# Correcting a planner's dependency and small-copy times in an attention-plus-Fourier kernel

## The chip, the cores and the metric

The kernel runs on one core of one Trainium2 chip. The metric is the device time of that core in microseconds, the median of several executions. One more execution was recorded by the hardware profiler; all rows of the trace come from that one.

## The reference

Two independent sublayers share the sequence length 2048 and the width 448, and their outputs stand side by side.

```python
# A: Fourier mixing, real part
a = jnp.einsum("bsd,ed->bse", x, dft_hid_re)
b = jnp.einsum("bsd,ed->bse", x, dft_hid_im)
y = jnp.einsum("ts,bse->bte", dft_seq_re, a) - jnp.einsum("ts,bse->bte", dft_seq_im, b)
# B: multi-head attention, H = 16 heads of 28
qkv = (x @ wqkv) ...                       # q, k, v by head
scores = jnp.einsum("bhqd,bhkd->bhqk", q, k) * 28 ** -0.5
p = softmax(scores, axis=-1)
o = einsum("bhqk,bhkd->bhqd", p, v) ... @ wo
return jnp.concatenate([y, o], axis=-1)
```

All is float32. To keep the precision, most operands are split into a rounded part (`hi`) and a rest (`lo`), and a product is made as hi x hi + lo x hi + hi x lo.

## The kernel before

**Two kinds of work on TensorE.** *Fill* work is all that has no softmax in it: the projections of q and k (`project`) and of v (`values`), matmuls of L547; the Fourier sublayer's hidden DFT (`hidden`, L547 too, twice: real and imaginary) and its sequence DFT (`sequence`, L662, 2 x 16 row tiles of 48 matmuls). *Attention* works in units of one head and 512 queries, 64 in all. A unit's 16 score tiles of 128 x 512 are made by L808 (`unit_kept`, 44 units) or twice by L754 and L786 (`unit_twice`, 20 units). P times V is L735, in narrow tiles of 32 columns, two groups a unit; L877 folds four partial sums in the same narrow mode.

**A unit of `unit_kept`.** ScalarE (ACT) copies each score tile out of PSUM (L415); VectorE (DVE) runs an elementwise maximum over the 16 tiles, each reading the last one's result (L815, then L818). Behind them stands a short dependent chain on VectorE: a transpose (L823), a reduction (L825), three 32x16 copies (L830), a small reduction (L835), two more small copies (L833) and a transpose (L841). ScalarE copies the result to SBUF as `mb` (L843); the pairs of score tiles are shifted by it, on GpSimd (POOL) or VectorE (L858), ScalarE takes the exponential (L862), and L735 multiplies by V. The sum leaves PSUM for `ou` by either ScalarE (L415) or VectorE (L417). In `unit_twice` VectorE reduces each tile to row maxima (L758, L762), a transpose on TensorE (L717) and two small operations (L766, L767) send the maxima through DRAM into two extra rows of q, and the second set of scores (L786) goes straight into the exponential (L790).

**Weight pieces.** `Piece` loads 256 KB of a weight or DFT matrix (L515, on the SP queue) into one of three `wraw` buffers; ScalarE casts it to `whi` (L516), GpSimd subtracts to get `wlo` (L522). `project`, `hidden` and `sequence` each make their pieces that way. Projection results are emptied from two fill banks by ScalarE (L588) and VectorE (L589); values by VectorE (L615), stored by L619.

**What sets the order.** Nothing is scheduled on the chip by time: every engine runs its instructions in the order in which they were emitted. That order comes from a planner in the kernel itself (`Schedule`). It plays the kernel through with a guessed cost for each operation: each engine, when free, takes the ready task with the smallest key (a due time), if its buffers are free. The constants that matter here: `DVE_P` 0.60 for a full VectorE operation, `SMALL` for the small copies of L830 and L833, `RAW` (passed as `own`) for the extra time until a VectorE operation that reads the last one's result may start, and for a DMA its size and an `extra` latency. A piece's key is the due time of its first matmul less a lead (9 for `hidden`, 12 for `sequence`, 12 for the projections). A changed constant changes the emitted order of all engines, and nothing else.

Of the kernel before, what the change touches and what calls it, by code (L numbers as in the profile page):

```python
# [47 lines left out]
def f32(ap):  # L48
    return ap.bitcast(F32)
# [4 lines left out]

RAW = 0.16
LANES = 8
FLOW, FLOW_IN = 200.0, 400.0
T_IN = 20.0  # L60
# [257 lines left out]
def tile_kernel(ctx, tc, xa, wre, wim, wd, xb, wqkv, wo, out):  # L318
    nc = tc.nc
# [67 lines left out]


    M512, M448, MS = 0.2335, 0.2065, 0.2365
    ACT_P, ACT_S, DVE_P, POOL_2, SMALL = 0.48, 0.52, 0.60, 1.25, 0.11  # L390

    def pe(key, emit, n=1, d=MS, lat=0.25, **kw):
        return sch.add({"PE": n * d}, key, emit, lat=lat, **kw)
# [1 line left out]
    def dma(key, emit, size=256, extra=0.0, n=1, **kw):  # L395

        return sch.add({"SP": 0.4}, key, lambda e: emit(), dmas=[(size, extra)] * n, **kw)
# [111 lines left out]
    class Piece:  # L509


        def __init__(self, src, key, kind="c", early=False):
            self.hi, self.lo = whi.slot(), wlo.slot()
            raw = wraw.slot()
            ld = dma(key, lambda: nc.sync.dma_start(raw.t, src()), acq=[raw])  # L515
            a = act(key + (0 if early else 1), lambda: nc.scalar.activation(self.hi.t, raw.t, AF.Copy), ACT_S,  # L516
                    deps=[ld], acq=[self.hi], use=[raw])
            at = key + (0 if early else 1.5)
            both = ("DVE",) if early else ("POOL",)
            e = {g: {"DVE": 0.8, "POOL": 1.25}[g] for g in both}  # L520
            n = 4 if kind == "c" else 3
            b = sch.add(e, at, lambda g: eng[g].tensor_tensor(  # L522
                self.lo.t[:, :n], raw.t[:, :n], f32(self.hi.t)[:, :n], op=ALU.subtract),
                deps=[a], acq=[self.lo], use=[raw, self.hi])
            self.ready, self.hi_ready, self.lo_ready = [b], a, [b]
            if kind == "x":
                self.ready.append(sch.add({g: {"DVE": 0.3, "POOL": 0.53}[g] for g in both}, at, lambda g: eng[g].tensor_tensor(
                    self.hi.t[64:, 3], raw.t[64:, 3], f32(self.hi.t)[64:, 3], op=ALU.subtract),
                    deps=[a], use=[raw, self.hi]))
            elif kind == "w":  # L530
                self.ready.append(sch.add({g: {"DVE": 0.3, "POOL": 0.53}[g] for g in both}, at, lambda g: eng[g].tensor_tensor(
                    self.lo.t[:64, 3], raw.t[:64, 3], f32(self.hi.t)[:64, 3], op=ALU.subtract),
                    deps=[a, b], use=[raw, self.hi, self.lo]))
                self.ready.append(sch.add({"DVE": 0.15, "POOL": 0.25}, at, lambda g: eng[g].memset(
                    f32(self.lo.t)[64:, 3], 0.0), deps=[b], use=[self.lo]))
                self.lo_ready = self.ready
# [89 lines left out]
    def hidden(part, weights, ready, after):  # L626
        done = []
        for st in range(NT):
            key = fkey(11, M448)
            w = Piece(lambda st=st: xa[st], key - 9, "x")  # L630
            o = fill_s.slot()
            seq = products(lambda k, w=w: (lambda: w.hi.t[:, k]), lambda k, w=w: (lambda: w.lo.t[:, k]),
                           lambda w=w: (lambda: w.hi.t[:, 3]), lambda k: (lambda: weights.h[:, k]), lambda k: (lambda: weights.l[:, k]))
            end = chain(key, seq, o, D, [*w.ready, *ready], [w.hi, w.lo], M448, weights.slots if st == NT - 1 else ())
            hi, lo = ab_h[:, st, :], ab_l[:, st, :]
            if part == 0:
                a = act(key - 10, lambda o=o, hi=hi: nc.scalar.activation(hi, o.t[:, :D], AF.Copy), 0.43, deps=[end, *after], use=[o])
                b = dve(key - 10, lambda o=o, hi=hi, lo=lo: nc.vector.tensor_tensor(
                    lo, o.t[:, :D], f32(hi), op=ALU.subtract), 0.54, deps=[a], use=[o])
            else:  # L640
                a = act(key - 10, lambda o=o, hi=hi: nc.scalar.activation(hi, o.t[:, :D], AF.Copy, scale=-1.0), 0.43,
                        deps=[end, *after], use=[o])
                b = dve(key - 10, lambda o=o, hi=hi, lo=lo: nc.vector.scalar_tensor_tensor(
                    lo, o.t[:, :D], -1.0, f32(hi), op0=ALU.mult, op1=ALU.subtract), 0.54, deps=[a], use=[o])
            done.append(b)
        return done

    def sequence(part, made):
        src = wim if part else wre
        for tt in range(NT):  # L650
            o, pair = fill_s.slot(), kept_s.slot()
            yo = Half(pair, 0)
            begun = None
            for q in range(4):
                key = fkey(12, M448)
                w = Piece(lambda tt=tt, q=q: src[tt, :, q * 4:q * 4 + 4, :], key - 12)
                for i in range(12):
                    k, j = divmod(i, 3)

                    def emit(e, k=k, j=j, q=q, w=w, o=o):  # L660
                        a, b = ((w.hi, ab_h), (w.hi, ab_l), (w.lo, ab_h))[j]
                        nc.tensor.matmul(o.t[:, :D], a.t[:, k, :], b[:, q * 4 + k, :], start=(q == 0 and k == 0 and j == 0),  # L662
                                         stop=(q == 3 and k == 3 and j == 2))
                    first = q == 0 and i == 0
                    deps = [last[0]]
                    if i == 0:
                        deps += w.ready
                    if tt == 0:
                        deps += [made[q * 4 + k]]
                    last[0] = pe(key + i * M448, emit, d=M448, deps=deps, acq=[o] if first else [],  # L670
                                 use=[w.hi, w.lo, *([] if first else [o])])
                    if i == 0 and q == Q_YO:
                        begun = last[0]
            key = key - 10
            if part == 0:
                b = dve(key, lambda o=o, yo=yo: nc.vector.tensor_copy(yo.t[:, :D], o.t[:, :D]), 0.53, deps=[last[0]], use=[o, pair])
                y_stored[tt] = dma(key, lambda yo=yo, tt=tt: nc.sync.dma_start(y_d[tt], yo.t[:, :D]), deps=[b], use=[pair])
            else:
                ld = dma(key - 15, lambda yo=yo, tt=tt: nc.sync.dma_start(yo.t[:, :D], y_d[tt]), deps=[y_stored[tt], begun], use=[pair])
                b = dve(key, lambda o=o, yo=yo: nc.vector.tensor_tensor(yo.t[:, :D], o.t[:, :D], yo.t[:, :D], op=ALU.add), 0.53,  # L680
                        deps=[last[0], ld], use=[o, pair])
                dma(key, lambda yo=yo, tt=tt: nc.sync.dma_start(out[tt * P:(tt + 1) * P, 0:D], yo.t[:, :D]), deps=[b], use=[pair])
# [112 lines left out]
    def unit_kept(u):  # L795
# [6 lines left out]
        for kt in range(NT):  # L802
# [11 lines left out]
            if kt == 1:  # L814
                prev = dve(key - 20, lambda o=o, s=kept[0]: nc.vector.tensor_tensor(rm.t, o.t, s.t[:, 0, :], op=ALU.max),  # L815
                           deps=[m, cs[0]], use=[rm, o, kept[0]], lock=[o], own=RAW)
            elif kt:
                prev = dve(key - 20, lambda o=o: nc.vector.tensor_tensor(rm.t, o.t, rm.t, op=ALU.max),  # L818
                           deps=[m, prev], use=[rm, o], lock=[o], own=RAW)
        key = t_a + 16 * dt - 20  # L820
# [4 lines left out]
        r = dve(key, lambda o=o: nc.vector.tensor_reduce(  # L825
            pm.t[:, :NT], o.t.rearrange("p (j r) -> p j r", r=32), axis=AX.X, op=ALU.max, negate=True), deps=[t], use=[o, pm], own=RAW)

# [4 lines left out]
        def back(n, o=o):  # L832
            return lambda: nc.vector.tensor_copy(o.t[n:2 * n, :NT], o.t[:n, :NT])  # L833
        r = [dve(key, beside(i), SMALL, deps=[r], use=[pm], own=RAW) for i in (1, 2, 3)]
        r = dve(key, lambda o=o: nc.vector.tensor_reduce(  # L835
# [81 lines left out]
    key = fkey(0, 0)  # L917
# [5 lines left out]
    key = fkey(0, 0)  # L923
# [19 lines left out]
    for n, c in enumerate(LAST):  # L943
        raws = []
        for k in range(4):
            pair = kept_s.slot()
            raw = Half(pair, 0)
            key = T_OUT + n
            deps = [o_done[h, c] for h in range(H) if (h + 1) * DH > k * P and h * DH < (k + 1) * P] + [before["ka"]]
            if k < 3:  # L950
                ld = dma(key, lambda raw=raw, k=k, c=c: nc.sync.dma_start(raw.t, on_d[k * P:(k + 1) * P, c * CH:(c + 1) * CH]),
                         deps=deps, use=[pair])
            else:
# [3 lines left out]
                ld = dma(key, twice, 128, n=2, deps=deps, use=[pair])  # L957
            raws.append((raw, ld))
        for i in range(2):
            x = [kt_s.slot() for _ in range(4)]  # L960
            ready = []
            for k in range(4):
                raw, ld = raws[k]
                src = lambda raw=raw, i=i: raw.t[:, i * HF:(i + 1) * HF]
# [3 lines left out]
                key = T_OUT + n + i / 2  # L968
# [7 lines left out]
            for t in range(2):  # L976
# [6 lines left out]
                key = T_OUT + 5 + (n * 4 + i * 2 + t) * 2.3  # L983
# [49 lines left out]
```

## Time and profile before

| | us |
|---|---|
| median of 3 runs | 1163.07 (1162.79 to 1165.32) |
| profiled execution, its own time | 1163.75 |
| its span | 1161.9 |
| busy: TensorE, VectorE, ScalarE, GpSimd | 1145.3, 1010.8, 1029.1, 884.6 |

A row of the profile names the line of the kernel, the engine, the operation, what it writes and reads, and how often; then the busy time, the mean duration in ns and the engine's idle time ahead of it, with what ended that. PE is TensorE's matmul, PEld its weight load, which runs ahead of the matmul. In timeline rows the first number is the start and the second the duration, in microseconds from the span's start. A matmul's duration includes the time it takes to drain; the next one starts before it ends. GpSimd's spans are rough.

### The profile page before, as it was taken

To read this page: it belongs to the slowest core of one execution; us is meant where nothing else is said; L and a number is where in the kernel's file an instruction comes from. 1 tells how busy PE (TensorE), PEld (TensorE's weight loads), DVE (VectorE), ACT (ScalarE), POOL (GpSimd) and SP (SyncE) were. 2 spreads that over 40 slices of the span, in tenths; PEclk is the share of its full clock that TensorE was granted. 3 is DMA by queue.
4 is the path that set the end of the run, shared out by engine and by line. 5 is a ranking of instruction groups with operands and counts; after the bars stand their busy time and mean duration, and the time that the engine had idled before them with its cause. 6 is when DMAs were issued, how large, how long until landed. Compare 5 with 4: busy or idle time off the path is not lost.

```text
span 1161.9 us, 19485 instructions
## 1 busy us (share of the span) xinstructions
PE 1145.3 (99%) x6110; PEld 778.7 (67%) x6110; DVE 1010.8 (87%) x1803; ACT 1029.1 (89%) x1748; POOL 884.6 (76%) x521
## 2 busy tenths in 40 slices
PE   8999999999999999999999999999999999999998
PEld 7876556656676667767666656566666667766677
DVE  6599989999898989999899999998989998799832
ACT  5269999999999899999899999999999999899952
POOL 2138687888789888978888897987989899596630
PEclk9999999999999999999999999999999999999999
DMA  8893344222223222232333232232423223323543
GB/s 259 176 214 120 125 140 148 66 83 73 82 85 102 85 85 82 73 114 78 89 105 100 86 96 65 85 101 90 120 80 96 88 87 114 120 73 92 162 158 109
DMA packets 111880, 125.19 MB, mean 108 GB/s; under 512 B 49368, under 2 KB 63352, under 8 KB 111776
## 3 DMA queue, kind: packets, MB, share of 16 engines
q1 hardware_dynamic: 111776, 123.94, 35.8%
q8 instruction: 48, 0.79, 0.3%
q14 instruction: 56, 0.46, 0.1%
HBM read 90.00 MB, written 33.77 MB: 107 GB/s over the span
## 4 chain that ended last, share of the span: by engine, by line
PE 79%; DVE 9%; ACT 5%; DMA 3%; issue 3%; SPq 0%; DVEq 0%; ACTq 0%
PE bank L662 25%; PE bank L735 17%; PE bank L808 13%; PE bank L547 8%; PE bank L786 6%; PE bank L754 5%; DVE rm L818 4%; PE bank L987 3%; ACT kept L415 2%; DMA kept<-xb 1%; PE bank L877 1%; DVE mx L758 1%; ACT kept L790 1%; ACT kept L862 1%; DVE bank L823 1%
## 5 line engine op out<-in xcount | busy, mean ns | idle before, releaser
L858 POOL TENSOR_TENSOR kept<-kept,mb 128x1024 f32<-128x1024 f32 x254 | 605.7, 2409 | 93.7 <-ACT mb L843 85.6
L818 DVE TENSOR_TENSOR rm<-bank,rm 128x512 f32<-128x512 f32 x616 | 421.7, 685 | 53.7 <-PE bank L808 17.3
L415 ACT ACTIVATE kept<-bank 128x512 f32<-128x512 f32 (+1 forms) x661 | 381.0, 625 | 59.4 <-PE bank L808 34.4
L862 ACT ACTIVATE kept<-kept 128x1024 f32<-128x1024 f32 x341 | 361.2, 1102 | 7.8 <-DVE kept L858 5.0
L662 PE MATMUL bank<-big,whi 128*128 128x448 f32 x1024 | 325.3, 368 | 0.0
L522 POOL TENSOR_TENSOR wlo<-wraw,whi 128x512 fp32r<-128x512 f32 (+1 forms) x166 | 204.2, 1233 | 131.3 <-ACT whi L516 94.8
L808 PE MATMUL bank<-q,k 84*128 84x512 f32 x704 | 277.2, 414 | 2.6 <-DVE bank L841 1.6
L735 PE MATMUL bank<-kept,v 128*32 128x512 f32 x1944 | 240.7, 597 | 1.3 <-DVE mx L758 0.7
L758 DVE TENSOR_REDUCE mx<-bank 128x1 f32<-128x512 f32 x320 | 216.0, 681 | 8.6 <-PE bank L754 7.2
L662 PEld LDWEIGHTS bank<-big,whi 128*128 128x128 f32 x1024 | 193.3, 189 | 32.4 <-issue 5.9
L662 PE MATMUL bank<-big,wlo 128*128 128x448 f32 x512 | 188.4, 368 | 0.2 <-POOL wlo L522 0.2
L808 PEld LDWEIGHTS bank<-q,k 84*128 84x128 f32 x704 | 130.1, 189 | 86.8 <-issue 19.5
L790 ACT ACTIVATE kept<-bank 128x512 f32<-128x512 f32 x290 | 179.3, 637 | 4.1 <-PE bank L786 3.5
L735 PEld LDWEIGHTS bank<-kept,v 128*32 128x32 f32 x1944 | 56.4, 109 | 123.7 <-issue 110.9
L786 PE MATMUL bank<-q,k 86*128 86x512 f32 x320 | 127.4, 408 | 0.7 <-DMA q<-nmd 0.6
L754 PE MATMUL bank<-k,q 84*128 84x512 f32 x320 | 127.3, 407 | 0.3 <-DVE n L767 0.3
L516 ACT ACTIVATE whi<-wraw 128x512 fp32r<-128x512 f32 x167 | 110.8, 667 | 15.3 <-DMA wraw<-wqkv 12.1
L858 DVE TENSOR_TENSOR kept<-kept,bank 128x1024 f32<-128x1024 f32 x87 | 104.1, 1210 | 5.3 <-ACT mb L843 4.9
L662 PEld LDWEIGHTS bank<-big,wlo 128*128 128x128 f32 x512 | 96.9, 189 | 14.5 <-issue 1.0
L547 PE MATMUL bank<-wd,whi 128*128 128x448 f32 x256 | 79.6, 373 | 1.4 <-ACT kept L415 1.1
L786 PEld LDWEIGHTS bank<-q,k 86*128 86x128 f32 x320 | 59.8, 188 | 31.5 <-DVE rm L818 8.1
L754 PEld LDWEIGHTS bank<-k,q 84*128 84x128 f32 x320 | 60.0, 188 | 26.5 <-issue 4.2
(81 smaller groups left out, 1081.1 us busy)
## 6 DMA issues: line engine op xcount, KB each, us to landing
wraw<-wre SPq DMA_DIRECT2D x64, 256.0 KB
wraw<-wim SPq DMA_DIRECT2D x64, 256.0 KB
qkd<-wd SPq DMA_DIRECT2D x32, 256.0 KB
wraw<-xa SPq DMA_DIRECT2D x32, 256.0 KB
k<-qkd SPq DMA_DIRECT2D x64, 112.0 KB
q<-qkd SPq DMA_DIRECT2D x64, 112.0 KB
qkd<-kept SPq DMA_DIRECT2D x24, 256.0 KB
out<-kept SPq DMA_DIRECT2D x27, 224.0 KB
```

The lines of the kernel that those rows point to most:

```text
L415: nc.scalar.activation(dst, src, AF.Copy)
L522: b = sch.add(e, at, lambda g: eng[g].tensor_tensor(self.lo.t[:, :n], raw.t[:, :n], f32(self.hi.t)[:, :n], op=ALU.subtract), deps=[a], acq ...
L662: nc.tensor.matmul(o.t[:, :D], a.t[:, k, :], b[:, q * 4 + k, :], start=(q == 0 and k == 0 and j == 0), stop=(q == 3 and k == 3 and j == 2))
L735: nc.tensor.matmul(o.t[j * VW:(j + 1) * VW, :], VT[h].t[:, kt // 4, j, :], pairs[i // 2].t[:, i % 2, :], start=(kt < 4), stop=(kt >= NT - 4))
L754: m = pe(key, lambda e, o=o, kc=kc, qt=qt: nc.tensor.matmul(o.t, q.t[:KR, qt * P:(qt + 1) * P], KT[h][kc].t[:KR, :], start=True, stop=True ...
L758: ms.append(dve(key - 20, lambda o=o, kc=kc, qt=qt: nc.vector.tensor_reduce(mx.t[:, qt, kc:kc + 1], o.t, axis=AX.X, op=ALU.max), deps=[m], ...
L786: m = pe(key, lambda e, o=o, kt=kt: nc.tensor.matmul(o.t, KT[h][kt // 4].t[:KR + 2, kt % 4 * P:(kt % 4 + 1) * P], q.t[:KR + 2, :], start=T ...
L790: es.append(act(key - 20, lambda o=o, p=p: nc.scalar.activation(p.t, o.t, AF.Exp, scale=SCALE), deps=[m], use=[o, p.pair]))
L808: m = pe(key, lambda e, o=o, kt=kt: nc.tensor.matmul(o.t, KT[h][kt // 4].t[:KR, kt % 4 * P:(kt % 4 + 1) * P], q.t[:KR, :], start=True, sto ...
L818: prev = dve(key - 20, lambda o=o: nc.vector.tensor_tensor(rm.t, o.t, rm.t, op=ALU.max), deps=[m, prev], use=[rm, o], lock=[o], own=RAW)
L858: eng[e].tensor_tensor(s.t, s.t, over_pair(pm.t if e == "DVE" else mb.t), op=ALU.add)
L862: es.append(act(key, lambda s=s: nc.scalar.activation(s.t, s.t, AF.Exp, scale=SCALE), 0.96, deps=[sh], use=[s]))
```

## The change

Three constants and two leads. `RAW` goes from 0.16 to 0.20 and `SMALL` from 0.11 to 0.21. Pieces with keys between 1 and 80 (those of the second and the third projection; the first has key 0.2, the fourth comes later than 80) are planned to land 6 us later. The pieces of `hidden` and `sequence` get keys 2 us earlier. No instruction is added or taken away: the planner sees other costs and emits another order.

```diff
-RAW = 0.16
+RAW = 0.20
...
-    ACT_P, ACT_S, DVE_P, POOL_2, SMALL = 0.48, 0.52, 0.60, 1.25, 0.11
+    ACT_P, ACT_S, DVE_P, POOL_2, SMALL = 0.48, 0.52, 0.60, 1.25, 0.21
...
-            ld = dma(key, lambda: nc.sync.dma_start(raw.t, src()), acq=[raw])
+            ld = dma(key, lambda: nc.sync.dma_start(raw.t, src()), extra=6 if 1 < key < 80 else 0.0, acq=[raw])
...
-            w = Piece(lambda st=st: xa[st], key - 9, "x")
+            w = Piece(lambda st=st: xa[st], key - 11, "x")
...
-                w = Piece(lambda tt=tt, q=q: src[tt, :, q * 4:q * 4 + 4, :], key - 12)
+                w = Piece(lambda tt=tt, q=q: src[tt, :, q * 4:q * 4 + 4, :], key - 14)
```

## The prediction

> **What bounds the kernel now.** I read the page's busy shares first, then the chain that ended last, then a table of stretches, and in each stretch who waited for whom.
>
> ```profile
> PE 1145.3 (99%) x6110; PEld 778.7 (67%) x6110; DVE 1010.8 (87%) x1803; ACT 1029.1 (89%) x1748; POOL 884.6 (76%) x521
> PE 79%; DVE 9%; ACT 5%; DMA 3%; issue 3%; SPq 0%; DVEq 0%; ACTq 0%
> ```
>
> TensorE is the bound: it is busy 99% of the span and makes 79% of the chain. The change removes no matmul, so it can pay only in the 1161.9 - 1145.3 = 16.6 us in which TensorE stands idle, and in the waits that its weight port (PEld) shows while the last matmuls drain. Where are they? In the stretches below the columns are: length, busy time of PE, PEld, DVE, ACT, POOL, granted clock, DMA share, GB/s.
>
> ```profile
> 80.00:300.00 220.00, 215.23 (x1101) 135.07 (x1100) 207.08 (x366) 207.83 (x356) 180.59 (x112) 0.99 0.33 109
> 300.00:650.00 350.00, 349.29 (x1931) 236.65 (x1929) 317.99 (x559) 330.88 (x557) 298.34 (x157) 1.00 0.30 91
> 650.00:800.00 150.00, 147.74 (x796) 96.46 (x795) 140.02 (x246) 145.85 (x253) 130.63 (x87) 1.00 0.29 86
> 800.00:1080.00 280.00, 279.97 (x1551) 187.11 (x1551) 253.31 (x442) 262.69 (x439) 237.68 (x128) 1.00 0.32 97
> ```
>
> TensorE idles 4.77 us at 80-300, 2.26 us at 650-800, and next to nothing elsewhere between 80 and 1080 (0.71 and 0.03 us). The share of VectorE (DVE) goes with it: 94.1% and 93.3% in the two stretches that idle, 90.9% and 90.5% in the two that don't. So where VectorE has no air, TensorE waits. Who holds its weight port at 80-300:
>
> ```profile
> PEld bank L808 <- DVE mx L758: 3.9, 10, 0.6
> PEld bank L808 <- DVE bank L841: 3.4, 7, 1.2
> PEld bank L717 <- DVE nm L762: 3.1, 3, 1.4
> PEld bank L754 <- DVE mx L758: 2.2, 5, 0.8
> ```
>
> That is 12.6 us of waits for VectorE (total, times, longest), among them L841 and L762, the ends of the two short chains behind a unit's scores. They bound from above what TensorE loses there to VectorE; the 4.77 us of idle TensorE bound it from below.
>
> **The planner's times against the trace.** `RAW` is the extra time between a VectorE operation and one that reads its result, `SMALL` the cost of a 32x16 or 64x16 copy.
>
> ```profile
> 576.62 0.68 DVE L758 TENSOR_REDUCE mx<-bank 128x1 f32<-128x512 f32 x1
> 577.22 2.27 DVE L818 TENSOR_TENSOR rm<-bank,rm 128x512 f32<-128x512 f32 x3
> ...
> 569.64 0.60 DVE L830 COPY bank<-bank 32x16 f32<-32x16 f32 x3
> ```
>
> An operation that needs nothing of the one ahead starts 0.60 us after it (576.62 to 577.22). Three maxima that each read the last one's result take 2.27 us, so with 0.68 for the last, (2.27 - 0.68) / 2 = 0.79 us each: the dependence costs 0.19, and 0.20 is nearer than 0.16. Three small copies take 0.60 us, with 0.18 for the last 0.21 each: 0.21 is right and 0.11 was half. The Trainium skill ("VectorE: DVE Perf Modes", The DRAIN you can't avoid) says the opposite of the first: eight copies took the same 13.88 us with a semaphore after each as with one at the end. By that rule dependence would cost nothing and the new plan would keep VectorE free in vain; the 0.79 against 0.60 here speaks against it, and the first rival below carries its chance.
>
> **Part 1, the first weight pieces planned 6 us later** (keys between 1 and 80: the pieces of the second and third projection). Rows of ScalarE (ACT), VectorE and TensorE:
>
> ```profile
> 26.62 0.63 ACT L516 ACTIVATE whi<-wraw 128x512 fp32r<-128x512 f32 x1 [7.04 <-DMA wraw<-wqkv]
> 28.96 0.63 ACT L516 ACTIVATE whi<-wraw 128x512 fp32r<-128x512 f32 x1 [1.72 <-DMA wraw<-wqkv]
> 29.50 1.06 ACT L588 ACTIVATE kept<-bank 128x512 fp32r<-128x512 f32 x2
> ...
> 30.11 1.29 DVE L589 TENSOR_TENSOR kept<-bank,kept 128x512 fp32r<-128x512 f32 x2 [5.69 <-ACT kept L588]
> ...
> 30.86 5.38 PE L547 MATMUL bank<-wd,big 128*128 128x448 f32 x25 [2.47 <-DVE kept L589]
> ```
>
> Two casts (L516) stand on ScalarE ahead of the copies (L588) that empty TensorE's two fill banks, and wait for their pieces. TensorE stops until L588 and L589 are through. In the new order the second L516 stands between the two L588; the DMA issues up to these pieces are the same, so they land as before. Then the first L588 starts after the first cast, at 26.62 + 0.54 = 27.16 (the L588 behind the second cast came 29.50 - 28.96 = 0.54 after it), and TensorE goes on 30.86 - 29.50 = 1.36 later, at 28.52 instead of 30.86: 2.3 us saved. What is late next is the other bank: its L588 runs at 29.50 as now, ready at 30.86, and the first bank's eleven matmuls take until 28.52 + 11 x 0.21 = 30.8 (25 of them took 5.38), so 0.1 us at most. On the SP queue two stores of V (L619) now stand ahead of the loads of the third and the fourth key chunk, and each waits for its VectorE copy:
>
> ```profile
> 35.66 0.62 DVE L615 COPY kept<-bank 128x448 f32<-128x448 f32 x1 [1.54 <-PE bank L547]
> ...
> 52.55 0.60 ACT L415 ACTIVATE kept<-bank 128x512 f32<-128x512 f32 x1 [1.24 <-PE bank L808]
> ```
>
> The later of them is through at 36.3, and the eighth score of the first unit, the last that reads the second chunk, is copied at 52.55: 16 us of cover, cost nothing. Bounds of this part: 0 (the pieces land later in this run) to 2.5.
>
> **Part 2, `RAW` and `SMALL` make a new order everywhere from about 40 us on.** I read both programs' instruction orders side by side, engine by engine. Over the whole kernel VectorE gives up 5 of its 89 pair shifts (L858) to GpSimd (POOL) and 15 of its 82 plain copies (L417) to ScalarE, 12 of them of `ou`; and L818 stands right behind the operation whose result it reads 201 times, not 238. Between the 272nd and the 674th fill matmul (L547 and L662 counted through), which the trace has at 80 and 300 us, it is 7 copies, 2 shifts and 10 such neighbours fewer; 8 maxima fewer too, but with them go their matmuls. The prices of copy and shift:
>
> ```profile
> L858 POOL TENSOR_TENSOR kept<-kept,mb 128x1024 f32<-128x1024 f32 x254 | 605.7, 2409 | 93.7 <-ACT mb L843 85.6 <-issue 4.4 <-ACT n L766 2.0
> L858 DVE TENSOR_TENSOR kept<-kept,bank 128x1024 f32<-128x1024 f32 x87 | 104.1, 1210 | 5.3 <-ACT mb L843 4.9
> L417 DVE COPY ou<-bank 128x512 f32<-128x512 f32 x45 | 30.7, 682 | 5.3 <-PE bank L735 5.1
> L415 ACT ACTIVATE ou<-bank 128x512 f32<-128x512 f32 x19 | 11.3, 597 | 8.6 <-PE bank L735 8.5
> ```
>
> 7 x 0.68 + 2 x 1.21 + 10 x 0.19 = 9.1 us off VectorE's 207.08: its share falls from 94.1% to 90.0%, that of the stretches where TensorE hardly idles. I take 6 us saved, nearer to the 4.77 of idle TensorE than to the 12.6 of port waits, since a port wait is partly hidden behind matmuls still running; bounds 0 and 10 (what the port waits leave hidden taken off). One more thing hangs on it:
>
> ```profile
> 280.00:300.00 20.00, 18.58 (x88) 12.26 (x87) 17.28 (x32) 18.22 (x32) 16.98 (x11) 0.91 0.21 71
> ...
> 287.91 0.50 PE L808 MATMUL bank<-q,k 84*128 84x512 f32 x1 [0.92 <-DVE bank L841]
> ```
>
> Around a 0.92 us wait for L841 the granted clock of these 20 us is 0.91, worth 0.09 x 20 = 1.8 us, part of the 6. The Trainium skill ("TensorE: Matmul & The Clock Gate", What's actually happening) lets the clock halve only after an idle window of about 3.4 us; the trace has no such gap here, so by the page the slow clock has another cause, these 1.8 us would stay, and the time would be that much longer.
>
> At 650-800 the same reading (one copy more, 2 shifts and 11 neighbours fewer, 3.8 us of 140.02) gives 90.8%; I take 1 of the 2.26 us.
>
> What it costs: TensorE enters the narrow matmuls (P.V, L735, and L877) 120 times, not 109.
>
> ```profile
> 95.02 1.85 PE bank L735 x16
> 164.49 3.57 PE bank L735 x32
> ...
> 116.78 1.92 PE L735 MATMUL bank<-kept,v 128*32 128x512 f32 x16
> 118.64 0.50 PE L786 MATMUL bank<-q,k 86*128 86x512 f32 x1
> 118.97 0.40 PE L808 MATMUL bank<-q,k 84*128 84x512 f32 x1
> ```
>
> A second group of 16 in the same visit adds 3.57 - 1.85 = 1.72, so going in costs 0.13. Coming out, the next matmul ends 119.14 - 118.70 = 0.44 after the run, and the one after that 119.37 - 119.14 = 0.23 later: 0.21 lost. Eleven more visits: 11 x 0.34 = 3.7 us, all on the engine that bounds. Bounds 2.3 (coming out alone) and 5.
>
> ScalarE gets 15 x 0.6 = 9 us and GpSimd 5 x 2.41 = 12 us. ScalarE is busy 89%, GpSimd idles 93.7 us ahead of its shifts, most of it for `mb`. I take nothing; bounds 0 and 6, by the second rival.
>
> **Part 3, later pieces due 2 us sooner.** In the order of before a sequence piece's `wlo` is made a median of 10 us of TensorE's work ahead of its first matmul, in the new one 9 to 10; three buffers hold it, not its due time.
>
> ```profile
> L662 PE MATMUL bank<-big,whi 128*128 128x448 f32 x1024 | 325.3, 368 | 0.0
> L662 PE MATMUL bank<-big,wlo 128*128 128x448 f32 x512 | 188.4, 368 | 0.2 <-POOL wlo L522 0.2
> ```
>
> TensorE waited 0.2 us for them in all. Worth nothing either way.
>
> **Sum.** -2.3 - 6 - 1 + 3.7 = -5.6. The profiled execution took 1163.75 us (span 1161.9 and 1.85 around it), 0.68 above the median of 1163.07 of the runs shown: 1163.75 - 5.6 = 1158.15, and against the median 1157.5.
>
> **Rivals.** *The middle gives nothing, the start pays for the visits:* TensorE's waits in the middle are not for want of VectorE but for the order's own unevenness, which a new order has elsewhere; then -2.3 + 3.7 = +1.4, 1164.5 against the median, and down to 1162 if a third of the 6 us comes after all. That dependence costs VectorE nothing would lead here too; 0.04 of this rival's chance is for it. For it: the port waits are many and small, none over 1.4 us. Against: they stand where VectorE's share is highest. *Slower, by ScalarE:* 12 more `ou` copies on ScalarE, each of which stops it until P.V ends. The 19 of now waited 8.5 us, 0.45 each, and behind them stand the copies that empty the score banks. 12 x (0.45 + 0.6) = 12.6 us on an engine at 89%. If half of it reaches TensorE, +6.3, and the middle's gain is gone: -2.3 + 3.7 + 6.3 = +7.7, 1171; with a third, 1168.6. It decides where ScalarE's share passes the 94.5% that 80-300 has now. Against: 28 us of air on ScalarE at 300-1080 (780 - 739.4 = 40.6 us less the copies' 12.6). *Larger gain:* the 12.6 us of port waits go for the most part: -2.3 - 10 - 2 + 3.7 = -10.6, 1152.5. *It does nothing:* hardly possible, the order differs on every engine from 40 us on.
>
> **Numbers.** Forecast 0.56, larger gain 0.12, nothing in the middle 0.17, slower by ScalarE 0.15. The first two are faster by over 0.2% (2.3 us, about what a measurement here can tell from no change): 0.68. The third is the same: 0.17; the last slower: 0.15. The range takes in the first three with their bounds and leaves out most of the last: 1151.5 to 1165.5.
>
> **What would show it.** Right: TensorE's wait at 28 us gone; idle TensorE at 80-300 under 2 us and VectorE's share there near 90%; 120 runs of narrow matmuls; L662 still without a wait. Wrong: PEld waits for ScalarE's L415 and L790 in place of those for VectorE; the granted clock under 1 in other places; TensorE idle at 28 us as before, if the pieces land later; or VectorE's share at 80-300 still near 94%.

## The result, and the profile after

The changed kernel is slower: a median of 1170.48 us (1166.38 to 1171.24, 7 runs) against 1163.49 us (1162.31 to 1165.55, 7 runs) of the kernel before on the same chip. The ratio is 1.0048, with a 95% interval of 1.0032 to 1.0064. The forecast was 1157.5 us with a range of 1151.5 to 1165.5, so it was wrong in sign and the time is outside its range. The profiled execution of after took 1170.52 us (span 1168.7), 6.77 more than the one of before.

The page of after, busy shares and shares of the chain:

```profile
PE 1147.0 (98%) x6110; PEld 784.5 (67%) x6110; DVE 1001.0 (86%) x1786; ACT 1035.1 (89%) x1763; POOL 895.9 (77%) x523
PE 84%; ACT 5%; DVE 5%; issue 2%; DMA 2%; SPq 1%; POOL 0%; DVEq 0%; ACTq 0%; POOLq 0%
```

The work moved as it was meant to: VectorE gives up 17 operations and 9.8 us, ScalarE and GpSimd take 15 and 2 more. TensorE's busy time has hardly changed, yet the span has grown by 6.8 us, so TensorE now stands idle for longer. The table of stretches says where (columns as in the prediction; first a stretch of before that was not shown, then after):

```profile
34.00:80.00 46.00, 45.85 (x210) 38.85 (x210) 34.41 (x83) 18.80 (x33) 4.61 (x4) 1.00 0.97 189
```

```profile
34.00:80.00 46.00, 39.70 (x172) 34.24 (x171) 26.62 (x67) 12.93 (x23) 1.64 (x3) 0.89 0.93 178
80.00:300.00 220.00, 215.39 (x1105) 139.61 (x1105) 204.35 (x365) 210.32 (x363) 176.66 (x107) 0.99 0.34 110
650.00:800.00 150.00, 149.72 (x815) 98.83 (x808) 139.82 (x245) 147.43 (x254) 138.05 (x90) 1.00 0.31 89
800.00:1080.00 280.00, 278.67 (x1535) 189.03 (x1537) 247.54 (x435) 263.35 (x446) 233.25 (x126) 1.00 0.31 95
```

Nearly all of the new idle time lies in one stretch, 34 to 80 us: TensorE is idle for 6.30 us instead of 0.15, makes 38 matmuls fewer and is granted a clock of 0.89. TensorE's timeline of after from 29 us on, and below it ScalarE's at 27 us, where the start was to change:

```profile
29.35 8.85 PE L547 MATMUL bank<-wd,big 128*128 128x448 f32 x42 [0.37 <-DVE kept L589]
...
38.04 0.40 PE L808 MATMUL bank<-q,k 84*128 84x512 f32 x1
38.28 0.37 PE L547 MATMUL bank<-wd,big 128*128 128x448 f32 x1
44.94 0.77 PE L754 MATMUL bank<-k,q 84*128 84x512 f32 x1 [6.30 <-DMA q<-qkd]
```

```profile
27.45 0.63 ACT L516 ACTIVATE whi<-wraw 128x512 fp32r<-128x512 f32 x1 [6.96 <-DMA wraw<-wqkv]
27.99 0.58 ACT L588 ACTIVATE kept<-bank 128x512 fp32r<-128x512 f32 x1
28.47 0.62 ACT L516 ACTIVATE whi<-wraw 128x512 fp32r<-128x512 f32 x1
29.07 0.60 ACT L588 ACTIVATE kept<-bank 128x512 fp32r<-128x512 f32 x1
```

The stop at 28 us has gone: 0.37 us instead of 2.47, with one L588 now between the two casts, as forecast (how far this wait varies is said below). In its place TensorE waits 6.30 us, once, for q of the first unit that is scored twice (L754). In before the first score of L754 ran at 39.78 us without a wait:

```profile
39.55 0.39 PE L808 MATMUL bank<-q,k 84*128 84x512 f32 x1
39.78 0.39 PE L754 MATMUL bank<-k,q 84*128 84x512 f32 x1
```

What q was waiting for shows on the queue of SP, first of before, then of after (start, time in the queue):

```profile
30.84 0.87 SPq L689 DMA_DIRECT2D k<-qkd  x1
32.65 0.33 SPq L690 DMA_DIRECT2D k<-qkd  x1
33.04 0.36 SPq L689 DMA_DIRECT2D q<-qkd  x1
33.45 0.38 SPq L690 DMA_DIRECT2D q<-qkd  x1
```

```profile
31.48 2.49 SPq L619 DMA_DIRECT2D vd<-kept  x2
34.06 1.08 SPq L689 DMA_DIRECT2D k<-qkd  x1
35.25 0.49 SPq L690 DMA_DIRECT2D k<-qkd  x1
35.84 0.35 SPq L592 DMA_DIRECT2D qkd<-kept  x1
36.24 0.41 SPq L593 DMA_DIRECT2D qkd<-kept  x1
39.28 0.87 SPq L689 DMA_DIRECT2D k<-qkd  x1
40.24 0.50 SPq L690 DMA_DIRECT2D k<-qkd  x1
40.84 0.34 SPq L592 DMA_DIRECT2D qkd<-kept  x1
41.26 0.38 SPq L593 DMA_DIRECT2D qkd<-kept  x1
41.69 0.46 SPq L689 DMA_DIRECT2D q<-qkd  x1
42.20 0.39 SPq L690 DMA_DIRECT2D q<-qkd  x1
```

In before, q's load is issued at 33.04, right behind the load of head 0's second key chunk. In after it is issued at 41.69, 8.65 us later, behind two stores of V (L619), two pairs of stores of projected rows (L592, L593) and the loads of head 0's second and third key chunks. The gap from 36.65 to 39.28 is the third chunk's load waiting until the stores ahead of it have landed in DRAM. q itself needs none of that. It only stands behind it.

The wait has a tail. The granted clock (last column but two) around it:

```profile
39.00:41.00 2.00, 0.00 (x0) 0.00 (x0) 0.00 (x0) 0.13 (x1) 0.00 (x0) 0.98 0.11 38
41.00:43.00 2.00, 0.00 (x0) 0.00 (x0) 0.00 (x0) 0.00 (x0) 0.00 (x0) 0.50 0.76 272
...
50.00:51.00 1.00, 1.00 (x4) 0.88 (x4) 0.35 (x1) 0.00 (x0) 0.00 (x0) 0.50 1.39 168
51.00:52.00 1.00, 1.00 (x5) 0.85 (x5) 0.52 (x4) 0.60 (x1) 0.00 (x0) 0.92 0.45 102
```

About 2.3 us into the wait the clock falls to 0.50, and it stays there until 51.1 us, 6.2 us after TensorE has gone on; at half speed that loses 3.1 us. Wait 6.3, slow clock 3.1, less the 2.1 saved at 28 us: +7.3, where the profiled execution is 6.77 longer. All the rest of the kernel, the part in which the planner's new times were to pay, comes to about nothing.

### The profile page after: what moved, and what is told of

It reads as the page before. It is cut to its first block, busy times and chain, and to the rows that moved or that the text cites. A ratio compares the mean times of both kernels' runs of the same rounds, so it can differ in the third digit from the quotient of the medians.

```text
span 1168.7 us, 19450 instructions
## 1 busy us (share of the span) xinstructions
PE 1147.0 (98%) x6110; PEld 784.5 (67%) x6110; DVE 1001.0 (86%) x1786; ACT 1035.1 (89%) x1763; POOL 895.9 (77%) x523
## 4 chain that ended last, share of the span: by engine, by line
PE 84%; ACT 5%; DVE 5%; issue 2%; DMA 2%; SPq 1%; POOL 0%; DVEq 0%; ACTq 0%; POOLq 0%
PE bank L662 24%; PE bank L735 18%; PE bank L808 14%; PE bank L547 12%; PE bank L786 6%; PE bank L754 6%; PE bank L987 3%; DVE rm L818 2%; ACT kept L415 2%; PE bank L877 1%; ACT kept L862 1%; DVE mx L758 1%; ACT kept L790 1%; DMA kept<-wqkv 1%; ACT whi L516 0%
## 5 line engine op out<-in xcount | busy, mean ns | idle before, releaser
L858 POOL TENSOR_TENSOR kept<-kept,mb 128x1024 f32<-128x1024 f32 x258 | 615.5, 2407 | 90.3 <-ACT mb L843 83.4
L862 ACT ACTIVATE kept<-kept 128x1024 f32<-128x1024 f32 x341 | 365.0, 1105 | 7.5 <-DVE kept L858 4.0
L662 PE MATMUL bank<-big,whi 128*128 128x448 f32 x1024 | 324.7, 368 | 0.0
L662 PEld LDWEIGHTS bank<-big,whi 128*128 128x128 f32 x1024 | 193.4, 189 | 29.5 <-issue 1.7
L662 PE MATMUL bank<-big,wlo 128*128 128x448 f32 x512 | 188.6, 368 | 0.1
L790 ACT ACTIVATE kept<-bank 128x512 f32<-128x512 f32 x284 | 174.8, 638 | 6.3 <-PE bank L786 5.9
L735 PEld LDWEIGHTS bank<-kept,v 128*32 128x32 f32 x1932 | 54.8, 109 | 123.8 <-issue 109.3
L754 PE MATMUL bank<-k,q 84*128 84x512 f32 x320 | 128.3, 408 | 6.8 <-DMA q<-qkd 6.3
L662 PEld LDWEIGHTS bank<-big,wlo 128*128 128x128 f32 x512 | 96.9, 189 | 16.7 <-issue 2.5
L858 DVE TENSOR_TENSOR kept<-kept,bank 128x1024 f32<-128x1024 f32 x83 | 99.7, 1211 | 4.9 <-ACT mb L843 4.7
L754 PEld LDWEIGHTS bank<-k,q 84*128 84x128 f32 x320 | 59.9, 189 | 35.5 <-DMA q<-qkd 6.7
L547 PE MATMUL bank<-wd,whi 128*128 128x448 f32 x256 | 82.2, 372 | 0.2 <-DVE big L638 0.2
```

The lines of the kernel that those rows point to most:

```text
L547: nc.tensor.matmul(o.t[:, :cols], w(), x(), start=(i == 0), stop=(i == n - 1))
L735: nc.tensor.matmul(o.t[j * VW:(j + 1) * VW, :], VT[h].t[:, kt // 4, j, :], pairs[i // 2].t[:, i % 2, :], start=(kt < 4), stop=(kt >= NT - 4))
L754: m = pe(key, lambda e, o=o, kc=kc, qt=qt: nc.tensor.matmul(o.t, q.t[:KR, qt * P:(qt + 1) * P], KT[h][kc].t[:KR, :], start=True, stop=True ...
L858: eng[e].tensor_tensor(s.t, s.t, over_pair(pm.t if e == "DVE" else mb.t), op=ALU.add)
L862: es.append(act(key, lambda s=s: nc.scalar.activation(s.t, s.t, AF.Exp, scale=SCALE), 0.96, deps=[sh], use=[s]))
```

## The experiments

Each kernel ran beside the kernel before on the same chip; the medians of before were 1164.59 us beside e1 to e4, 1164.99 beside e5 to e8 and 1165.22 beside e9 to e11. A gain or loss in us is the ratio's part of that. The theory after the result: the later pieces (`extra`) alone make the whole loss, by moving q on the SP queue. The rival: the new times (`RAW`, `SMALL`) make it, by ScalarE or by a worse order.

**e1_extra_alone.** Before, with the 6 us of `extra` and nothing else; TensorE's order differs from before in two places and ScalarE's in two, all of them in the start, as are the places on the other engines.

```diff
-            ld = dma(key, lambda: ..., acq=[raw])
+            ld = dma(key, lambda: ..., extra=6 if 1 < key < 80 else 0.0, acq=[raw])
```

> The kernel before with one edit: the pieces of the second and the third projection planned 6 us later. Theory (the load of the first unit's second q, L689, now stands behind stores on the SP queue and costs TensorE its 6.3 us wait at 38 to 45 us and some 2 us of slow clock after it): that wait is here too, the stop at 28 us is gone, and the time is 4 to 7 us over the kernel before, about 1169. Rival (the head of the kernel has air, and the loss comes from the new order of the middle and the end): within 2 us of the kernel before.

Measured: 1170.26 us, ratio 1.0043 (1.0025 to 1.0060), +5.0 us. The waits of TensorE between 20 and 60 us:

```profile
PE bank L754 <- DMA q<-qkd: 6.4, 1, 6.4
PE bank L547 <- DVE kept L589: 0.4, 1, 0.4
```

The same wait, as long as in after (6.3), with the middle's order untouched. The later pieces alone make as much as the whole change.

**e2_all_but_extra.** After, without the `extra`: new `RAW`, `SMALL` and leads.

```diff
-            ld = dma(key, ..., extra=6 if 1 < key < 80 else 0.0, acq=[raw])
+            ld = dma(key, ..., acq=[raw])
```

> The changed kernel without the 6 us for the first pieces: RAW, SMALL and the two leads as changed. Theory: no wait for q at 38 us, the stop at 28 us back, and the middle as in the changed kernel: 0 to 4 us under the kernel before, 1159.5 to 1163.5. Rival (the new middle costs by itself: eleven more visits to the narrow matmuls, a later end): 2 to 5 us over the kernel before.

Measured: 1163.84 us, ratio 0.9998 (0.9983 to 1.0012). The two constants and the two leads together are worth nothing that shows; the interval leaves room for under 2 us either way.

**e3_after_q_first.** After, with q of that one unit given a key that puts its load ahead; the orders of VectorE, ScalarE and GpSimd are those of after, TensorE's differs in two places, SP's in seven.

```diff
-        return [dma(due[u][0] - 12, lambda: rows_of(q.t, ...
+        return [dma(-50.0 if u == (0, 1) else due[u][0] - 12, lambda: rows_of(q.t, ...
```

> The changed kernel with one edit: the q load of the first twice-scored unit gets a key of -50, so that it is issued as soon as its rows are stored, ahead of the stores of V and of the third chunk of keys. Theory: the 6.3 us wait and the slow clock behind it go, 7 to 9 us less than the changed kernel, 1161 to 1163, and the stop at 28 us stays away. Rival (another load takes the place of q's, or the middle eats the gain): under 3 us less than the changed kernel.

Measured: 1161.89 us, ratio 0.9979 (0.9966 to 0.9992). Against after's 1.0048 that is 0.69%, 8.0 us, for seven places on one queue and two on TensorE. Its issue and TensorE's rows:

```profile
32.62 0.33 SPq L689 DMA_DIRECT2D q<-qkd  x1
```

```profile
38.15 0.40 PE L808 MATMUL bank<-q,k 84*128 84x512 f32 x1
38.38 0.40 PE L754 MATMUL bank<-k,q 84*128 84x512 f32 x1
```

q is issued at 32.62, and L754 follows its neighbour without a wait. It also settles the rival of ScalarE: with the same order on ScalarE as in after, the kernel is faster than before.

**e4_raw17.** A control for re-planning as such: `RAW = 0.17` instead of 0.16, a change too small to mean anything by itself.

> A change of no meaning: the kernel before with RAW 0.17 for 0.16. It shows what a new order does by itself. If the planner's costs mattered as the prediction has it, this hundredth would move the time by under 1 us; if each new order draws its waits anew, it moves it by 2 us or more in either direction, and the middle's change in the changed kernel is of the same kind.

Measured: 1167.44 us, ratio 1.0028 (1.0013 to 1.0043): +3.3 us for another order with no better reason. Its profiled execution (1163.98) was its fastest, so its trace does not show where the 3.3 us lie; that stays open.

**e5_extra_q_first.** e1 and e3's edit together, on before: the later pieces with q on time. TensorE's order is that of before.

> The kernel before with the first pieces planned 6 us later and the first twice-scored unit's q load given the key -50; RAW, SMALL and leads as before. Theory (the start is worth what the stop at 28 us costs once q is on time, and the middle and the end stay those of before): 1.5 to 2.5 us under the kernel before, no slow clock at 70 to 82 us, and no 1.9 us wait of L735 near the end. Rival (what the start saves is taken back by VectorE at 80 to 300, which is as loaded as before): within 1 us of the kernel before.

Measured: 1161.28 us, ratio 0.9975 (0.9961 to 0.9989): -2.9 us. The start is worth about what was forecast for it (-2.3) once q does not pay for it. That rests on the timed runs: in e5's profiled execution (1163.28, 2.0 over its median) TensorE still waited 2.05 us at L589.

**e6_raw_alone, e7_small_alone, e8_leads_alone.** Before, with one of the other three edits each: `RAW = 0.20`; `SMALL = 0.21`; leads 11 and 14.

> The kernel before with RAW 0.20 alone. Theory (RAW takes neighbours apart and so the waits of 80 to 300; the stretch at 70 to 82 us stays that of before, as its order has the same 29 VectorE instructions there): 0 to 3 us under the kernel before, less the price of 8 more visits to the narrow matmuls. Rival (a new order draws its waits anew, as RAW 0.17 did): 1 to 4 us over it.

> The kernel before with SMALL 0.21 alone. Its order has 33 VectorE instructions against 29 between the 225th and the 272nd fill matmul. Theory: it alone brings the slow stretch of 70 to 82 us (fewer than 22 matmuls in each 6 us, granted clock near 0.75 in one of them), 2 to 3 us; with what it gains at 80 to 300 it comes out at -1 to +2 us. Rival (RAW or the leads bring the slow stretch): clock 1.00 there.

> The kernel before with the two leads alone, 11 and 14 for 9 and 12. Prediction: worth nothing by themselves, as the pieces were never waited for; within 1 us of the kernel before if the order's change does nothing. Rival (a new order draws its waits anew): 1 to 4 us away from it in either direction, with L662 as free of waits as before.

Measured: e6 1171.26 us, ratio 1.0059 (1.0039 to 1.0079), +6.9; e7 1170.18 us, 1.0041 (1.0024 to 1.0059), +4.8; e8 1164.79 us, 1.0001 (0.9983 to 1.0018), nothing. Each constant alone, corrected to what the trace shows, costs; both with the leads cost nothing (e2). The parts do not add up: +6.9 + 4.8 + 0.1 against -0.2. e6's theory missed, and its rival had the direction but not the size; e7's had the slow stretch below and missed the time. Most of the loss lies at the end of the traces (e6's profiled execution is near its median, e7's was its slowest). The stretch from 1080 to 1130 us, of before, of e6, of e7:

```profile
1080.00:1130.00 50.00, 49.84 (x267) 35.60 (x266) 30.59 (x53) 37.19 (x68) 22.05 (x15) 1.00 0.54 169
```

```profile
1080.00:1130.00 50.00, 47.16 (x227) 29.90 (x226) 31.09 (x47) 35.96 (x61) 22.19 (x15) 0.93 0.51 158
```

```profile
1080.00:1130.00 50.00, 45.34 (x241) 28.71 (x234) 34.56 (x51) 36.66 (x63) 26.75 (x18) 0.97 0.52 163
```

TensorE is idle for 2.84 us in e6 and 4.66 in e7, against 0.16, and the clock takes 0.07 x 50 = 3.5 and 0.03 x 50 = 1.5 us more: 6.3 and 6.2 us. The longest waits there are L877's for the copy of `ou` on VectorE, 2.0 us in e6 and two in e7 (before has no wait over 0.2):

```profile
PE bank L877 <- DVE ou L417: 4.7, 2, 2.7
```

A second place is the stretch at 76 to 82 us, first of before, then of e7, then of e11, a run with `SMALL` 0.21 that is told below:

```profile
76.00:82.00 6.00, 6.00 (x26) 4.39 (x25) 6.00 (x11) 5.16 (x10) 6.00 (x3) 1.00 1.02 377
```

```profile
76.00:82.00 6.00, 5.27 (x14) 3.54 (x14) 5.97 (x11) 4.35 (x8) 3.83 (x2) 0.76 0.80 292
```

```profile
76.00:82.00 6.00, 6.00 (x27) 4.64 (x26) 6.00 (x10) 4.95 (x9) 6.00 (x3) 1.00 1.00 363
```

e7 makes 14 matmuls there instead of 26, under a clock of 0.76; e6 is as before (27). e2 has the slow clock too (21 matmuls, 0.73). e11 has e2's order there and, like e2, idles 0.72 us just ahead (70 to 76 us), yet its clock stays at 1.00. So the idle time comes with `SMALL`; the slow clock behind it, the larger part, came in some executions and not in all.

**e9_q_first_alone.** The control to e5: q first on before, without later pieces.

> Control: the kernel before with the q load's key of -50 alone. Every engine but SP has the order of before. Theory (q was in time in the kernel before, and the gain of the runs with both edits comes from the stop at 28 us): within 1 us of the kernel before. Rival (the early q load itself saves): 2 us or more under it.

Measured: 1164.96 us, ratio 0.9997 (0.9983 to 1.0010). q on time is worth nothing where it was on time; e5's gain is that of the pieces.

**e10_extra8_q_first, e11_after_extra8_q_first.** Before and after, each with q first and 8 us of `extra` instead of 6, which puts the first bank's L588 ahead of both casts.

> The kernel before with the first pieces planned 8 us later, not 6, and the q load first. Now the first of the two L588 stands ahead of both casts and the second behind both. Theory (the stop at 28 us is L588 standing behind a piece's landing): the bank that TensorE needs first no longer waits for any landing, so the stop at 28 to 33 us goes to under 1 us in the profile and the time is 2.5 to 4.5 us under the kernel before. Rival (the other bank's L588, behind both casts, stops TensorE one chain later): no better than with 6 us.

> The changed kernel with the first pieces planned 8 us later, not 6, and the q load first. Theory: as the changed kernel with q first, less what the earlier L588 saves, 3 to 5 us under the kernel before. Rival (the middle and the end of the changed order are worse than those of before by what the start saves): 1 to 2 us under it.

Measured: e10 1161.56 us, ratio 0.9970 (0.9954 to 0.9986), -3.5 us; e11 1162.96 us, 0.9971 (0.9957 to 0.9984). The casts' piece lands late in e10's profiled execution, and TensorE's row shows that it no longer matters:

```profile
26.98 0.60 ACT L588 ACTIVATE kept<-bank 128x512 fp32r<-128x512 f32 x1 [6.03 <-PE bank L547]
29.16 0.63 ACT L516 ACTIVATE whi<-wraw 128x512 fp32r<-128x512 f32 x1 [1.57 <-DMA wraw<-wqkv]
```

```profile
31.96 4.35 PE L547 MATMUL bank<-wd,big 128*128 128x448 f32 x20 [0.33 <-DVE kept L589]
```

Both beat both kernels. With them there are three pairs that differ by `RAW`, `SMALL` and the leads alone, at three states of the start: e2 and before (0.9998 and 1), e3 and e5 (0.9979 and 0.9975), e11 and e10 (0.9971 and 0.9970). Each time the planner's corrected times are worth nothing that these runs can tell, which is to within about 2 us.

## Why the prediction was wrong

**The step that failed is Part 1's walk along the SP queue.** It named two stores of V moved ahead of two loads of keys, found 16 us of cover for these, and stopped there. A third load had moved past the same stores and past more besides: q's. Its last issue began at 33.45 in before, and from there the load takes 2.61 us (in the chain of after, from 42.20), so it lay ready at 36.06, and L754 reads it at 39.78: 3.7 us of cover. The last issue moved from 33.45 to 42.20, by 8.75, and TensorE comes to L754 1.1 us earlier, at 44.94 - 6.30 = 38.64: 8.75 - 3.7 + 1.1 = 6.15 us, and 6.30 was measured. The delay could not be read from the trace of before, but the cover could, and a cover of 3.7 us against a queue that waits for two VectorE copies and a landing should have set the range. Every bound of the start had been for a gain of 0 to 2.5; none was for a loss.

The two loads of keys were also taken for the wrong chunks. They are the third and the fourth load of keys on the queue, but by the emitted order they hold the second chunks of heads 0 and 1. The first unit's fifth score, at 46.65 in before, is the first to read head 0's second chunk, so the cover was 10 us, not 16. That it costs nothing held all the same: in e3 this load is issued later than in after (37.04 against 34.06), and TensorE doesn't wait for it.

**The start's own term held, its close size in part by luck.** -2.3 was forecast. 2.1 us of wait went in after's trace, and e5 and e10 measured -2.9 and -3.5, e9 0. But one pair of traces could not size it, as the wait differs between executions. Its longest stretch was 1.0 us (e2, e4) to 2.8 (e7, e9) with the pieces planned as in before, 0.4 (after, e1) to 2.1 (e5) with 6 us more, and 0.3 and 0.5 (e10, e11) with 8. Behind three of the longer ones (e6, e8, e9) the clock fell to 0.50 for 3.4 us, 1.7 us more, which the term didn't have. e3, 8.0 us faster than after by one key, shows the right term that the missing one had hidden.

**The middle: the sum about right in the traces, its reading wrong, the two edges missing.** To compare the stretches I counted, matmul by matmul, how much later each one ends than its usual spacing behind the one ahead (0.206 us for a 448-wide, 0.235 for a 512-wide, 0.108 for a narrow one); idle time, slow clock and the way in and out of narrow groups are all in it. Between 80 and 1080 us before loses 53.5 us and after 49.5: -4.0, where the forecast had -6 - 1 + 3.7 = -3.3. It is no accident of one execution: before's order there loses 51.7 to 54.8 us in five executions (before, e1, e5, e9, e10), after's 47.7 to 50.0 in four (after, e2, e3, e11). But in e2 and e3, where the start's wait doesn't stand ahead of it, 34 to 80 us loses 2.9 more than before (the thin stretch at 70 to 82 us; in e11, without the slow clock, 1.4 more), and the end from 1080 on loses 2.2 and 2.1 more (after 3.6). No term of the sum had a place there. The end's wait in after:

```profile
PE bank L735 <- ACT kept L862: 1.7, 1, 1.7
```

e2 has the same row. So what the middle gains is given back at its two edges, and the timed runs of e2, e3 and e11 against their partners say that nothing is left that they can tell.

**The signs that were to show the middle right didn't come.** VectorE's share at 80 to 300 was to fall to 90.0% and idle TensorE under 2 us; the share fell to 204.35 / 220 = 92.9% and 4.61 us stay. And the reading beneath, that TensorE waits where VectorE has no air, falls with the experiments; e6 and e7 in the same stretch:

```profile
80.00:300.00 220.00, 216.23 (x1113) 135.68 (x1112) 207.20 (x367) 209.18 (x358) 178.96 (x109) 1.00 0.34 111
```

```profile
80.00:300.00 220.00, 215.77 (x1109) 138.18 (x1111) 201.35 (x358) 209.56 (x361) 177.94 (x110) 0.99 0.34 112
```

The first is e6, the second e7: 3.77 us idle with VectorE at 94.2%, 4.23 us idle with 91.5%. Four stretches of one order had suggested a rule that other orders don't keep; that the middle's -4.0 lies near the forecast's -3.3 is therefore luck. One account, which no run here isolates: ten operations fewer is an average, TensorE waits for single ones, and which wait comes last is dealt anew by each plan. A change of 0.01 in `RAW` moved the kernel by 0.28% (e4); a sum of that size can claim little.

**The other points.** 120 visits to the narrow matmuls were counted ahead and run, at 0.34 us each. L662 waits as little as before:

```profile
L662 PE MATMUL bank<-big,wlo 128*128 128x448 f32 x512 | 188.6, 368 | 0.1
```

So Part 3's nothing holds, and e8 measured it. The rival *slower, by ScalarE* gave 1171, near the result, but by another mechanism: ScalarE's `ou` copies did wait longer (13.2 us in 14 waits, 8.5 before), and e3 keeps all of them and gains. *The middle gives nothing* was right on the middle, in the timed runs. Neither says anything of q.

**The clock.** After's rows show 0.50 from 2.3 us into a 6.3 us wait until 6.2 us after it. The Trainium skill ("TensorE: Matmul & The Clock Gate", What's actually happening) lets the clock halve after an idle window of about 3.4 us and come back after a busy window of that length, and says that this window runs freely. The half agrees; the fall came sooner here. One busy window at half speed would cost 3.4 / 2 = 1.7 us, an estimate. In e1 the same wait cost 1.6 us, as the clock was back 3.2 us after it; in after it cost 3.1. The prediction's doubt was about a slow clock without such a gap, and there are several. Behind waits of 2.5 to 2.8 us the clock fell in e6, e8 and e9 and did not in before and e7. In e7 it averages 0.76 between 76 and 82 us while TensorE idles 6.00 - 5.27 = 0.73 us in all. Each of these slow stretches, and the one that the prediction read at 280 to 300 us, lasted 3.4 us; e1's lasted 6.7 and after's 10.2, two and three times that. A window that runs freely would look so, but why one short wait is followed by a slow clock and the next is not, no run here isolates.

What stays open: why `RAW` alone and `SMALL` alone lose 6 us and more at the end, and both with the leads about 2. The place and the waits are shown, in one profiled execution of each; which decision of the planner leads there was not tried.

## What to carry to other kernels

When an order changes, walk each DMA queue by itself and list every load that moved, with its first reader and its cover; a load inherits all the waits of what stands ahead of it on its queue, needed or not (here 8.65 us on the queue became 6.3 us of TensorE and 3.1 us of slow clock). A planner's constant that is truer is not a better order: run a null change of the same kind first (here 0.28% for 0.01) and credit only what exceeds it and holds at several starting points. Where a sum of parts comes out at zero, take the parts singly: this change held a gain of 3 us and a loss of 8, and one key kept the gain.

## What the runs showed of the hardware

VectorE's subtraction of 128x256 (L411), which reads two inputs from SBUF, takes 0.41 us each when GpSimd is idle. Beside a GpSimd operation on two SBUF inputs (L858) it can take as long as that operation. VectorE and GpSimd of after:

```profile
1108.20 0.99 DVE L411 TENSOR_TENSOR k<-kept,k 128x256 fp32r<-128x256 f32 x1
1109.11 2.59 DVE L411 TENSOR_TENSOR k<-kept,k 128x256 fp32r<-128x256 f32 x1
1111.63 0.75 DVE L411 TENSOR_TENSOR k<-kept,k 128x256 fp32r<-128x256 f32 x2
```

```profile
1108.87 2.56 POOL L858 TENSOR_TENSOR kept<-kept,mb 128x1024 f32<-128x1024 f32 x1
```

GpSimd's operation ends at 1108.87 + 2.56 = 1111.43. The VectorE operation that started beside it ends 0.27 us later, at 1111.70; the two after it run with GpSimd idle. The Trainium skill ("GPSIMD Engine Reference", Specifications) has the two engines share their SBUF interfaces, with contention where a VectorE instruction has two SBUF inputs. The rows agree, and give a price: up to 2.59 us instead of 0.41. The planner's one duration for a VectorE operation cannot know it.
